# Attention with float32 scores on half arrays and V as the stationary operand, from inputs that the host lays out

## Chip, cores and metric

One core of one Trainium2 chip runs the whole program. The metric is the device time of one execution in microseconds. The engines are TensorE (PE; PEld is its weight load), VectorE (DVE), ScalarE (ACT), GpSimd (POOL) and SyncE (SP), whose queue issues the transfers.

## What is computed

Attention with a block-causal mask over 8 batches of 8 heads, 576 tokens of 64 columns, then a soft mixture of experts over the 4608 tokens, then a wide layer with squared ReLU whose weights are float64.

```python
scores = scale * np.matmul(q, k.transpose(0, 1, 3, 2))      # (8, 8, 576, 576)
mask = block_i >= block_j                                   # blocks of 64 tokens
scores = np.where(mask, scores, -1000000000.0)
attn = np.exp(scores - np.max(scores, axis=-1, keepdims=True))
attn = attn / (np.sum(attn, axis=-1, keepdims=True) + 1e-09)
x = np.matmul(attn, v)                                      # then to (4608, 512)
x = _moe_ref(x=x, **moe_kwargs)
return _moe2_ref(x=x, **moe2_kwargs)
```

## The kernel before

Attention goes over 32 pairs of heads (p), four pairs a batch. A pair's two heads lie on the two halves of the partitions, 64 columns each. A plan written out by hand sets the order: `SLOT` gives each step a time in a pair's own clock of 8 units (L24), the steps of all pairs are sorted by 8p plus that time, and each engine executes its part of the sorted list in order (`run`, L608). A step that waits therefore holds all that stands behind it on its engine.

The steps of a pair. `load` (L228) brings q and k in rows and v (eight transfers for q and k, three for v). `t_kq` transposes q and k on TensorE, ten transposes of 128 columns (L274). `c_kq` copies them on ScalarE rounded to float32r (KQ, L282), and `d_kq` keeps what the rounding lost on VectorE (KQL, L287). `rough` (L298) computes scores from the rounded parts alone and `rough_max` (L307) takes each row's maximum on VectorE; `m_row` (L325) transposes the maxima and two transfers put them into one row per head, MR. `score` (L370) goes over four chunks `CH` of key blocks and query columns (448, 448, 320+128 and 192+128 columns a head); each chunk takes four single passes: high by high, high by low, low by high, and NEG by MR, which subtracts the maxima and sets masked entries. `expo` takes the exponential on ScalarE (L384), `p_hi` a float16 part of it on ScalarE, `p_lo` the float16 remainder on GpSimd (L391). `v_scale` and `split_v` scale V by a power of two and split it in two float16 parts (L333, L349). `pv` (L407) multiplies in three float16 products for each block of 128 queries, 128 keys and head, 90 in all, with the weights as the stationary operand and V, with a column of ones for the sums, streaming. `norm` (L421) divides on VectorE. `route_t` and the routing steps of a batch (L445 to L553) follow with transposes and small float32 products.

The banks: scores and rough scores share two buffers of two banks in turn (`ps_s`), transposes, maxima and routing share two single banks (`ps_t`), and there is one buffer of two banks for the weights times V (`ps_v`).

After the last pair come the last batch's routing, the experts while the float64 weights are converted, and the wide layer, from L620 on. Their weights go into buffers that lie where the attention's tiles lay.

## Time and profile before

| what | us |
|---|---|
| median of 3 runs (971.98 to 978.46) | 974.12 |
| the profiled execution: its span | 974.9 |
| TensorE busy in it | 877.6 |
| VectorE busy | 699.4 |
| ScalarE busy | 599.5 |
| GpSimd busy | 286.1 |

The profiled execution has no time of its own beside its span, which is the time from its first to its last instruction. Busy times are averages over stages with different limits. A row of the timeline gives start and length; since matmuls are pipelined, the distance between two starts is what one costs and the length is what its result takes. A float32 product (not float32r) has two records on TensorE.

### The profile page before, as it was taken

What the parts mean: (1) busy time and instruction counts of PE and PEld (TensorE: products, weight loads), DVE (VectorE), ACT (ScalarE), POOL (GpSimd) and SP (SyncE); (2) the same over time, 40 slices, a digit from 0 to 9 for tenths busy, and PEclk for the clock granted to TensorE, in tenths of its full rate; (3) what the DMA queues carried; (4) which work ended last, traced back from release to release, by engine and by line L of the source; (5) the groups of instructions that cost most, each with busy time, mean ns of one, the idle gap of its engine ahead of it and who ended that gap; (6) DMA issues with size and microseconds to landing.
All of it is one profiled execution on the core that took longest, in us unless ns stands there. A gap on an engine that the chain in (4) does not pass through costs nothing.

```text
span 974.9 us, 20485 instructions
## 1 busy us (share of the span) xinstructions
PE 877.6 (90%) x8052; PEld 519.8 (53%) x8052; DVE 699.4 (72%) x1277; ACT 599.5 (61%) x1025; POOL 286.1 (29%) x224
## 2 busy tenths in 40 slices
PE   3899989988899989976857799999999999999998
PEld 2677767767677767763111344444444444444443
DVE  5798979878798979857978776565555565565553
ACT  2677767767677857774457565555555565555553
POOL 6476746656466656670100000000000000000000
PEclk9999999999999999996879799999999999999999
DMA  4544543535244424255998000001000100010001
GB/s 112 127 92 117 132 113 71 133 101 123 65 122 124 124 57 124 70 215 196 414 403 326 1 1 33 33 1 34 33 1 33 33 33 1 33 33 1 34 33 32
DMA packets 150927, 91.73 MB, mean 94 GB/s; under 512 B 127472, under 2 KB 127792, under 8 KB 150832
## 3 DMA queue, kind: packets, MB, share of 16 engines
q1 hardware_dynamic: 150832, 90.44, 30.8%
q8 instruction: 63, 1.03, 0.4%
q14 instruction: 32, 0.26, 0.1%
HBM read 80.81 MB, written 9.44 MB: 93 GB/s over the span
## 4 chain that ended last, share of the span: by engine, by line
PE 43%; DVE 7%; ACT 2%; issue 1%; DVEq 0%; ACTq 0%
PE o L1044 13%; PE o L1042 13%; PE o L1043 13%; PE h L1014 3%; DVE cvg L637 2%; DVE cve L644 1%; DVE cvg L636 1%; ACT cvl L728 1%; DVE cvl L645 1%; DVE wi L762 1%; DVE cvg L724 1%; PE h L657 0%; ACT wo_0s L745 0%; ACT cvg L633 0%; DVE wo_6s L750 0%
## 5 line engine op out<-in xcount | busy, mean ns | idle before, releaser
L263 POOL TENSOR_TENSOR pl<-pc,ph 128x896 f16<-128x896 f32 (+1 forms) x128 | 232.8, 1820 | 153.8 <-ACT ph L256 81.0
L1022 DVE SCALAR_TENSOR_TENSOR g<-r,sk 128x384 f32<-128x384 f32 x192 | 119.5, 622 | 126.0 <-ACT r L1016 124.4
L1016 ACT ACTIVATE r<-h,fo 128x384 f32<-128x384 f32 x192 | 111.3, 580 | 155.2 <-PE h L1014 154.0
L384 ACT ACTIVATE pc<-s 128x896 f32<-128x896 f32 (+1 forms) x128 | 110.7, 865 | 79.0 <-PE s L379 49.6
L1030 DVE SCALAR_TENSOR_TENSOR rl<-g,bk,rh 128x384 f16<-128x384 f32 x192 | 118.2, 615 | 8.9 <-ACT rh L1028 7.7
L1028 ACT ACTIVATE rh<-g,bk 128x384 f16<-128x384 f32 x192 | 116.2, 605 | 0.2 <-DVE g L1022 0.2
L256 ACT CAST ph<-pc 128x896 f16<-128x896 f32 (+1 forms) x128 | 113.4, 886 | 4.1
L293 DVE TENSOR_REDUCE mm<-s 128x2 f32<-128x1024 f32 (+3 forms) x128 | 101.9, 818 | 10.0 <-PE s L304 9.6
L780 POOL TENSOR_TENSOR c<-lgs,mc 128x192 f32<-128x192 f32 x6 | 3.7, 612 | 352.8 <-DVE mc L778 352.8
L417 PE MATMUL pv<-vh,ph 128*128 128x65 f16 x960 | 103.0, 197 | 1.3 <-DVE xt L433 1.3
L419 PE MATMUL pv<-vh,pl 128*128 128x65 f16 x960 | 101.5, 194 | 1.4 <-POOL pl L263 1.4
L418 PE MATMUL pv<-vl,ph 128*128 128x64 f16 x960 | 101.8, 194 | 0.0
L417 PEld LDWEIGHTS <-ph 128*128 128x128 f16 x960 | 86.9, 98 | 23.4 <-issue 6.4
L1044 PEld LDWEIGHTS <-rl 128*128 128x128 f16 x576 | 56.4, 98 | 68.9 <-DVE rl L1030 1.0
L1042 PEld LDWEIGHTS <-rh 128*128 128x128 f16 x576 | 56.5, 98 | 66.5 <-issue 0.3
L419 PEld LDWEIGHTS <-pl 128*128 128x128 f16 x960 | 88.9, 98 | 1.6 <-POOL pl L263 1.5
L418 PEld LDWEIGHTS <-ph 128*128 128x128 f16 x960 | 88.9, 99 | 0.0
L1043 PEld LDWEIGHTS <-rh 128*128 128x128 f16 x576 | 56.5, 98 | 58.2 <-issue 0.6
L263 DVE TENSOR_TENSOR kql<-tp,kq 128x512 fp32r<-128x512 f32 (+1 forms) x96 | 57.5, 600 | 30.2 <-ACT kq L285 29.2
L269 PE MATMUL tp<-idF,rqk 128*128 128x128 f32 x320 | 58.5, 301 | 22.0 <-DVE kql L263 9.6
L304 PE MATMUL s<-kq 64*128 64x64 f32 (+4 forms) x384 | 55.9, 338 | 19.8 <-DVE me L293 13.8
L379 PE MATMUL s<-mr,neg 64*128 64x128 f32 (+3 forms) x384 | 66.7, 318 | 6.7 <-DMA mr<-mT 6.5
(229 smaller groups left out, 1963.6 us busy)
## 6 DMA issues: line engine op xcount, KB each, us to landing
w<-in_moe_w_dram SPq DMA_DIRECT2D x36, 512.0 KB
w2h<-in_moe_w_dram SPq DMA_DIRECT2D x28, 512.0 KB
rqk<-in_k_dram SPq DMA_DIRECT2D x64, 128.0 KB
rqk<-in_q_dram SPq DMA_DIRECT2D x64, 128.0 KB
rv<-in_v_dram SPq DMA_DIRECT2D x64, 128.0 KB
wi<-in_moe_w_in_dram SPq DMA_DIRECT2D x8, 1024.0 KB
wo<-in_moe_w_out_dram SPq DMA_DIRECT2D x8, 1024.0 KB
out_dram<-ob SPq DMA_DIRECT2D x32, 256.0 KB
```

The costliest lines, as they stand in the source:

```text
L256: ACT.copy(o, i)
L263: eng.tensor_tensor(out=o, in0=i, in1=h, op=ALU.subtract)
L417: PE.matmul(o, a, vh[:, 2 * sl + h, 0:65], start=(c == 0 and n == 0), stop=False)
L418: PE.matmul(o[:, 0:64], a, vl[:, 2 * sl + h, :], start=False, stop=False)
L419: PE.matmul(o, l, vh[:, 2 * sl + h, 0:65], start=False, stop=(c == 3 and n == len(UNIT[c]) - 1))
L1016: ACT.activation(out=r, in_=hps, func=AF.Relu, scale=fo[:, 0:1])
L1022: DVE.scalar_tensor_tensor(out=g0, in0=r, scalar=sk[:, f:f + 1], in1=r, op0=ALU.mult, op1=ALU.mult)
L1028: ACT.activation(out=rh, in_=g0, func=AF.Identity, bias=bk[:, f:f + 1])
L1030: DVE.scalar_tensor_tensor(out=rl, in0=g0, scalar=bk[:, f:f + 1], in1=rh, op0=ALU.add, op1=ALU.subtract)
L1042: PE.matmul(o, rh[:, 128 * i:128 * i + 128], hl[f][0], start=(f == 0), stop=False)
L1043: PE.matmul(o, rh[:, 128 * i:128 * i + 128], hl[f][1], start=False, stop=False)
L1044: PE.matmul(o, rl[:, 128 * i:128 * i + 128], hl[f][0], start=False, stop=(f == 15))
```

## The change

The host passes k and q transposed, two heads on 128 rows and 640 columns, and v with its rows in place and zeros at the end, so that each is one transfer. The transposes of q and k, both remainders, the scaling and the splits go. q and k are rounded to float32r by ScalarE for the rough scores alone (`round_kq`). The scores are one float32 product on the unrounded data and the NEG by MR pass. V in float32 is the stationary operand, 64 columns for each head, and the float32 weights stream; the two heads write the two halves of the output's partitions. The result, columns by tokens, is copied out by ScalarE (`pv_out`), transposed on TensorE (`tokens`), and `norm` divides it. The sums of the weights over the key blocks are made on GpSimd (`key_sum`), split in two float16 parts by ScalarE and GpSimd (`sum_hi`, `sum_lo`), and summed over the keys by products with a column of ones (`dens`). The plan has new times.

```diff
 SLOT = {
-    "ld_k": -28.8, "ld_q": -28.6, "ld_v": -18.0,
-    "t0": -17.0, "c0": -16.98, "d0": -16.97, "t1": -15.2, "c1": -15.1, "d1": -15.05, "t2": -13.2, "c2": -13.1, "d2": -13.0,
+    "ld_k": -17.7, "ld_q": -17.6, "ld_v": -10.0, "rd_k": -13.6, "rd_q": -13.4,
     "r0": -11.8, "x0": -11.6, "r1": -9.8, "x1": -9.6, "r2": -7.8, "x2": -7.6, "r3": -5.8, "x3": -5.6,
-    "m_row": -3.2, "vs0": -9.3, "vs1": -5.1, "sv0": -4.5, "sv1": -2.5,
+    "m_row": -3.2,
     "s0": 0, "e0": 0.1, "s1": 2, "e1": 2.1, "s2": 4, "e2": 4.1, "s3": 6, "e3": 6.1,
-    "h0": 0.3, "h1": 2.3, "h2": 4.3, "h3": 6.3, "l0": 0.5, "l1": 2.5, "l2": 4.5, "l3": 6.5,
-    "pv0": 4.7, "pv1": 6.7, "pv2": 8.7, "pv3": 10.7, "norm": 10.9,
+    "a0": 0.3, "a1": 2.3, "a2": 4.3, "a3": 6.3, "sh0": 4.6, "sh1": 8.3, "sl0": 6.4, "sl1": 8.4,
+    "pv0": 2.7, "pv1": 4.7, "pv2": 6.7, "pv3": 8.7, "oc": 8.9, "tb0": 10.75, "tb1": 11.3, "den": 11.35, "norm": 11.4,
...
     def load(p, nm):
...
+        t = {"k": KT, "q": QT, "v": RV}[nm][p % 3]
+        SP.dma_start(out=t, in_={"k": k, "q": q, "v": v}[nm][p // 4, p % 4])
...
-    def t_kq(p, x):
-    def c_kq(p, x):
-    def d_kq(p, x):
+    def round_kq(p, nm):
+        o, i = (KR, KT) if nm == "k" else (QR, QT)
+        cp(RND[nm], o[p % 2], i[p % 3])
...
-        [(3, 384, 576, 0), (4, 448, 576, 192)],
+        [(3, 384, 576, 0), (4, 512, 576, 192)],
...
     def score(p, c):
-            for n, (a, b) in enumerate([(t[:, 0, ks], t[:, 1, qs]), (t[:, 0, ks], l[:, 1, qs]), (l[:, 0, ks], t[:, 1, qs]),
-                                        (NEG[:, sl, :], mr[:, qs])]):
+            for n, (a, b) in enumerate([(kt[:, ks], qt[:, qs]), (NEG[:, sl, :], mr[:, qs])]):
                 for h in range(2):
...
+    def key_sum(p, c):
+        pc = st["pc", p, c]
+        if c == 0:
+            return
+        if c == 1:
+            S = st["S", p] = ring("S", [128, 2, 448], F32)
+            POOL.tensor_tensor(out=S, in0=st["pc", p, 0], in1=pc, op=ALU.add)
+            return
+        S = st["S", p]
+        for sl, c0, c1, o in CH[c]:
+            if sl:
+                x = S[:, :, c0 - 128:c1 - 128]
+                POOL.tensor_tensor(out=x, in0=x, in1=pc[:, :, o:o + c1 - c0], op=ALU.add)
+
+    def sum_hi(p, part):
...
+            ACT.copy(st["sh", p][:, :, 0:128], st["pc", p, 2][:, :, 320:448])
...
+            ACT.copy(st["sh", p][:, :, 128:576], st["S", p])
+
+    def sum_lo(p, part):
...
+            lo(POOL, st["sl", p][:, :, 128:576], st.pop(("S", p)), st["sh", p][:, :, 128:576])
...
     def pv(p, c):
+        pc, rv = st["pc", p, c], RV[p % 3]
+        for sl, c0, c1, o in CH[c]:
+            head = sl == 0
+            x = (1, slice(0, c1)) if c1 <= 128 else (0, slice(c0 - 128, c1 - 128))
+            for h in range(2):
+                r = slice(64 * h, 64 * h + 64)
+                PE.matmul(st["pv", p][r, x[0], x[1]], rv[:, sl, r], pc[:, h, o:o + c1 - c0],
+                          start=head, stop=(sl == 4 or c1 <= 128))
+
+    def pv_out(p):
+        o, ps = ring("ot", [128, 576], F32), st.pop(("pv", p))
+        ACT.copy(o[:, 0:128], ps[:, 1, 0:128])
+        ACT.copy(o[:, 128:576], ps[:, 0, 0:448])
...
+    def tokens(p, part):
+        ot = st["ot", p]
+        ps = st["tb", p, part] = ps_t.tile([128, 512], F32, tag="tp", name="tp")
+        for n, u in enumerate(range(4) if part == 0 else (4,)):
+            tr(ps[:, 128 * n:128 * n + 128], ot[:, QS[u]:QS[u] + 128], idF)
+
+    def dens(p):
+        ps = st["tb", p, 1]
+        sh, sl = st.pop(("sh", p)), st.pop(("sl", p))
+        for u in range(5):
+            for h in range(2):
+                for n, x in enumerate((sh, sl)):
+                    PE.matmul(ps[:, 128 + 2 * u + h:129 + 2 * u + h], x[:, h, QS[u]:QS[u] + 128], ones_h[:, 0:1],
+                              start=(n == 0), stop=(n == 1))
...
-    at(-60, 0, build_zero)
...
+def _lay_k(a):
+    a = a.transpose(0, 1, 3, 2)
+    b, h, d, n = a.shape
+    a = a.reshape(b, h // 2, 2 * d, n)
+    return _concat([a, a[..., n - 64:]])
```

## Rows read from the trace of the kernel before

**Rows 1.** Attention's stretch: us; PE, PEld, DVE, ACT, POOL busy (instructions); clock; DMA share, GB/s.

```profile
0.00:437.18 437.18, 381.00 (x5653) 303.00 (x5653) 360.37 (x680) 303.19 (x482) 273.17 (x205) 0.98 0.44 111
```

**Rows 2.** The same columns for a regular pair and for the last pair.

```profile
281.03:292.67 11.64, 10.45 (x172) 8.69 (x169) 10.88 (x19) 9.12 (x15) 8.10 (x5) 1.00 0.37 84
...
428.87:437.18 8.31, 5.85 (x125) 5.12 (x121) 2.12 (x5) 5.77 (x8) 7.04 (x5) 1.00 1.02 414
```

**Rows 3.** Line L430 (norm): duration ns, first and last start.

```profile
L430 DVE TENSOR_TENSOR xb<-pv,rr x32: 691/692/692, 47.0 to 437.2; 128x512 f32<-128x512 f32 x32
```

**Rows 4.** Timeline of TensorE in a regular pair: start, us, line, tiles, shape, count.

```profile
275.46 0.82 PE L379 MATMUL s<-mr,neg 64*128 64x448 f32 x2
276.79 0.52 PE L304 MATMUL s<-kq 64*128 64x192 f32 x4 [0.50 <-DVE me L293]
277.24 0.20 PE L417 MATMUL pv<-vh,ph 128*128 128x65 f16 x1
...
277.98 0.63 PE L269 MATMUL tp<-idF,rqk 128*128 128x128 f32 x4
278.54 0.47 PE L379 MATMUL s<-kq 64*128 64x448 f32 x2
278.84 0.36 PE L379 MATMUL s<-kql,kq 64*128 64x448 f32 x2
...
279.46 0.19 PE L304 MATMUL s<-kq 64*128 64x64 f32 x2
...
281.34 0.28 PE L379 MATMUL s<-kq,kql 64*128 64x128 f32 x2
281.45 0.27 PE L379 MATMUL s<-mr,neg 64*128 64x128 f32 x2
281.94 0.50 PE L304 MATMUL s<-kq 64*128 64x512 f32 x2 [0.21 <-ACT kq L285]
```

**Rows 5.** Waits from 200 to 400 us: total, times, longest.

```profile
PE s L304 <- DVE me L293: 6.8, 9, 1.0
```

**Rows 6.** Timeline of TensorE: float32 products on 32 output columns, and what follows.

```profile
253.17 1.07 PE L516 MATMUL tp<-xb,d 128*32 128x512 f32 x8
254.06 1.02 PE L519 MATMUL tp<-xt,d 128*32 128x512 f32 x2
255.01 0.47 PE L379 MATMUL s<-kq 64*128 64x448 f32 x2
```

**Rows 7.** Groups of instructions, shapes apart: busy us, mean ns, idle before.

```profile
L263 POOL TENSOR_TENSOR pl<-pc,ph 128x896 f16<-128x896 f32 x96 | 182.1, 1898 | 129.5 <-ACT ph L256 64.8 <-issue 42.6 <-PE tp L269 9.4
L256 ACT CAST ph<-pc 128x896 f16<-128x896 f32 x96 | 90.2, 939 | 3.1
...
L357 DVE SCALAR_TENSOR_TENSOR vl<-rv,al,vh 128x640 f16<-128x640 f32 x32 | 64.7, 2021 | 1.0 <-POOL vh L354 1.0
...
L285 ACT CAST kq<-tp 128x512 fp32r<-128x512 f32 x64 | 36.8, 576 | 21.6 <-PE tp L269 21.1
```

**Rows 8.** Timeline of ScalarE in the same pair.

```profile
274.07 0.73 ACT L256 CAST ph<-pc 128x640 f16<-128x640 f32 x1
274.70 0.73 ACT L337 ACTIVATE sq<-rv 128x640 bf16<-128x640 f32 x1
...
279.72 0.92 ACT L384 ACTIVATE pc<-s 128x896 f32<-128x896 f32 x1 [0.49 <-PE s L304]
```

**Rows 9.** Timeline of VectorE at the start: the last mask copy and what follows.

```profile
13.78 1.52 DVE L224 CAST mr<-xb 64x640 fp32r<-64x640 f32 x2 [1.47 <-POOL xb L216]
15.34 1.29 DVE L263 TENSOR_TENSOR kql<-tp,kq 128x512 fp32r<-128x512 f32 x2
```

**Rows 10.** Timeline of TensorE at the start: the first pass with the maxima.

```profile
29.22 1.59 PE L379 MATMUL s<-mr,neg 64*128 64x448 f32 x2 [1.28 <-DMA mr<-mT]
```

**Rows 11.** Timeline of SyncE's queue: the row of maxima.

```profile
273.23 1.50 SPq L331 DMA_DIRECT2D mr<-mT  x2
```

**Rows 12.** Timeline of TensorE at the end of an odd batch.

```profile
350.96 0.66 PE L269 MATMUL tp<-idF,rqk 128*128 128x128 f32 x4 [2.02 <-ACT lp L494]
```

More of the change, by code (lines that the diff above doesn't have):

```diff
@@ L34 @@
 }
-PH = "AAAA"
-PL = "PPPP"
-LN256 = 5.545177444479562
+RND = {"k": "A", "q": "A"}
+PEXP = 16.0
+LNP = 2.772588722239781
 @with_exitstack
@@ L58, in fused_kernel @@
     PE, ACT, DVE, POOL, SP = nc.tensor, nc.scalar, nc.vector, nc.gpsimd, nc.sync
-    B, H, S, D = q.shape
+    B, D, S, H = q.shape[0], q.shape[2] // 2, q.shape[3] - 64, 2 * q.shape[1]
     NB = B
@@ L118, in fused_kernel @@
     idH = const.tile([128, 128], F16, name="idH")
-    ones_b = const.tile([128, 128], BF16, name="ones_b")
+    ones_h = const.tile([128, 2], F16, name="ones_h")
     I8 = const.tile([128, 64], F32, name="I8")
@@ L176, in fused_kernel @@
     ps_v = rt.enter_context(tc.tile_pool(name="ps_v", bufs=1, space=PSUM))
-    VH = [latep.tile([128, 10, 66], F16, name=f"vh_{i}") for i in range(3)]
     MX = [latep.tile([128, 128], F32R, name=f"mx_{i}") for i in range(2)]
@@ L182, in fused_kernel @@
     ME = [latep.tile([128, 2, 5], F32, name=f"me_{i}") for i in range(2)]
-    RS = [latep.tile([128, 2, 5], F32, name=f"rs_{i}") for i in range(2)]
+    RS = [latep.tile([128, 10], F32, name=f"rs_{i}") for i in range(2)]
     def load_const():
@@ L409, in pv @@
             st["pv", p] = ps_v.tile([128, 2, 512], F32, tag="pv", name="pv")
-        vh, vl = VH[p % 3], st["vl", p]
-        ph, pl = st.pop(("ph", p, c)), st.pop(("pl", p, c))
-        for h in range(2):
-            for n, (u, sl, off) in enumerate(UNIT[c]):
-                o = st["pv", p][:, h, 65 * u:65 * u + 65]
-                a, l = ph[:, h, off:off + 128], pl[:, h, off:off + 128]
-                PE.matmul(o, a, vh[:, 2 * sl + h, 0:65], start=(c == 0 and n == 0), stop=False)
-                PE.matmul(o[:, 0:64], a, vl[:, 2 * sl + h, :], start=False, stop=False)
-                PE.matmul(o, l, vh[:, 2 * sl + h, 0:65], start=False, stop=(c == 3 and n == len(UNIT[c]) - 1))
+        pc, rv = st["pc", p, c], RV[p % 3]
@@ new lines, in fused_kernel @@
+    QS = [128 * u for u in range(4)] + [448]
+    def tokens(p, part):
[11 more added lines that the diff above has]
+                              start=(n == 0), stop=(n == 1))
@@ new lines, in norm @@
+        rr = ring("rr", [128, 5, 2, 1], F32)
+        DVE.reciprocal(out=rr.rearrange("p u h a -> p (u h a)"), in_=r)
+        xo = XB[:, :, 128 * j:128 * j + 128].rearrange("p u (h c) -> p u h c", h=2)
+        DVE.tensor_tensor(out=xo, in0=t0.rearrange("p (u h c) -> p u h c", u=4, h=2),
+                          in1=rr[:, 0:4].to_broadcast([128, 4, 2, 64]), op=ALU.mult)
+        xt = XT[l0:l0 + 64, 128 * j:128 * j + 128].rearrange("p (h c) -> p h c", h=2)
+        DVE.tensor_tensor(out=xt, in0=t1[64:128, 0:128].rearrange("p (h c) -> p h c", h=2),
+                          in1=rr[64:128, 4].to_broadcast([64, 2, 64]), op=ALU.mult)
@@ L436, in gt @@
+        for c in range(4):
+            st.pop(("pc", p, c))
+        st.pop(("ot", p))
     def gt(b, i=0):
@@ L568, in fused_kernel @@
             A("ld_" + nm, load, nm)
-        for x in range(3):
-            A(f"t{x}", t_kq, x)
-            A(f"c{x}", c_kq, x)
-            A(f"d{x}", d_kq, x)
+        for nm in "kq":
+            A("rd_" + nm, round_kq, nm)
         for r in range(4):
@@ L583, in fused_kernel @@
             A(f"e{c}", expo, c)
-            A(f"h{c}", p_hi, c)
-            A(f"l{c}", p_lo, c)
+            A(f"a{c}", key_sum, c)
             A(f"pv{c}", pv, c)
+        for x in range(2):
+            A(f"sh{x}", sum_hi, x)
+            A(f"sl{x}", sum_lo, x)
+            A(f"tb{x}", tokens, x)
+        A("oc", pv_out)
+        A("den", dens)
         A("norm", norm)
@@ L1092, with _lay_q, _lay_v, _concat @@
 _OUTS = [((4608, 512), 'float32')]
+def _lay_k(a):
[3 more added lines that the diff above has]
+    return _concat([a, a[..., n - 64:]])
+def _lay_q(a):
+    a = a.transpose(0, 1, 3, 2)
+    b, h, d, n = a.shape
+    a = a.reshape(b, h // 2, 2 * d, n)
+    return _concat([a[..., :64], a])
+def _lay_v(a):
+    b, h, n, d = a.shape
+    o = np.zeros((b, h // 2, 640, 2, d), a.dtype)
+    o[:, :, :n] = a.reshape(b, h // 2, 2, n, d).transpose(0, 1, 3, 2, 4)
+    return np.ascontiguousarray(o.reshape(b, h // 2, 5, 128, 2 * d).transpose(0, 1, 3, 2, 4))
+def _concat(parts):
+    return np.ascontiguousarray(np.concatenate(parts, axis=-1))
+_LAY = {"q": _lay_q, "k": _lay_k, "v": _lay_v}
 def kernel(**inputs):
```

133 lines of the change are left out of this document (27 added, 106 removed).

## Prediction

> **What bounds the kernel now.** I read first the busy time of the attention stage, then single pairs, then one pair on TensorE, and last who waits for whom. Attention runs to 437.2 us of the 974.9; the change touches no code after it, so I leave those 537.7 us as they are. The reader is to see that in this stage, 32 pairs of heads, TensorE is busy 381 and VectorE 360 us [rows 1], and that neither has room: in a regular pair of 11.64 us TensorE is busy 10.45 and VectorE 10.88 [rows 2]. The normalisation runs once per pair, first at 47.0 and last at 437.2 [rows 3], so 31 intervals make 390.2 us. Of these 28 have the regular pair's length plus what a batch adds, and the last three are shorter, down to 8.31 [rows 2], for no rough maxima and transposes of a next pair are left.
>
> On TensorE the pair has 10.1 us of work and two waits. The rough scores that should follow the last pass at 275.46 start at 276.79, 1.1 us later than a pass's 0.2 us would give, and VectorE releases them; the ones at 281.94 come 0.4 us late [rows 4]. Over 200 us the VectorE wait stands at 6.8 us, longest 1.0 [rows 5]. So the pair is TensorE's work plus waits for a VectorE that is itself full.
>
> **TensorE's work after the change.** All float32 prices come from products that write 32 of the 128 output columns: four products of 512 columns, two records each, take 0.89 us (253.17 to 254.06), one alone 0.95 with what follows it [rows 6]. So a record of 512 columns streams 0.43 us, a product takes two records, and products on different column parts of the array run side by side. Per column that is 1.67 ns a product: 448 columns 0.75, 320 columns 0.54, 192 columns 0.32, 128 columns 0.22 us. I take the same overlap for two halves of the array; what happens otherwise is the first rival.
>
> Scores: a chunk of 448 columns now takes 0.92 us (278.54 to 279.46), 0.30 for the first pass and 0.20 for each other [rows 4]; after the change 0.10 exposed load, 0.75 and 0.20, together 1.05. For the other two a pass of 320 columns counts 0.15 by its columns and a narrow one 0.11 (281.34 to 281.45), which I take for 64 columns too. The chunk of 320 and 128 then stays at 1.12, the last, 192 and 64 instead of 192 and 128, goes from 0.97 to 0.86. Sum: +0.15.
>
> Weights times V: 24 products take 0.74 us (277.24 to 277.98) [rows 4], so 90 take 2.75. After: columns 448, 448, 320+128 and 192+64, so 0.75, 0.75, 0.76 and 0.43, 2.7 us, plus for each chunk a load that nothing hides and a change of the array's shape. The first pass of a score chunk is 0.1 us longer than the others, and at 255.01 the next shape starts 0.09 us after the float32 stream before it should end (254.06 and two records of 0.43) [rows 4, 6]; I take 0.15 for both (from nothing to 0.3). Sum 3.3: +0.55.
>
> Transposes: ten of q and k (0.56 for four [rows 4]) and the sum of squares go, 1.5 us; five of the output come (0.7) and 20 products of one column at 0.03 each, as the old products (0.6); with a change of shape 1.4: -0.05. Together 10.1 + 0.65 = 10.8 us: TensorE gets no relief.
>
> **The other engines.** VectorE loses the low half of V, 2.0 us [rows 7], and three remainders, 0.65 each for the wide ones [rows 9], some 4 of 10.88 us, and stops being late with what is left. ScalarE: from 9.1 to about 7.2 us. GpSimd: an 896-wide sum costs 1.90 us [rows 7]; with widths 896, 640, 384, 128, 256 and 896, at the same price per element (2.1 ns), 6.8 us, and 7.4 with an estimated 0.1 for each start. It fits in place of the 8.1 of today [rows 2]. Loads: one transfer instead of eight for q and k and three for v; the queue has less to issue and I count no gain.
>
> **The new waits.** Now ScalarE's order counts: weights of chunk 0, high half of the last pair's sums (896 wide), then the two copies that free the one output bank, and TensorE needs that bank for chunk 0 of the weights times V. From the end of the scores: 0.26 until ScalarE starts (279.46 to 279.72), then the chain. A ScalarE operation that doesn't read the one before starts about 0.1 us before its end (274.07 + 0.73 against 274.70) [rows 4, 8]. So 0.83 for the weights (0.92 long), 0.85 for the high half (0.94 [rows 7]), 0.15 and 0.53 for copies of 128 and 448 columns (a copy of 512 takes 0.58 [rows 7]), 0.06 back: 2.7 us. In this time TensorE has rough scores (0.45), the last weights times V (0.58), must wait for the weights of chunk 0 until 1.24, and does scores (1.05) and rough scores (0.12): 2.4. It waits 0.2 and 0.3, so the pair takes 10.8 + 0.5 = 11.3 us, 0.35 less than 11.64. Behind the waiting product stand the transposes, the sums' products and the scores of chunk 2. The sums' low half on GpSimd (1.90 after the high half, done 3.8 us after the scores) is read 4.25 us after them: hidden, by under half a us, and every tenth it is later costs a tenth. The row of maxima: two issues take 1.5 us [rows 11] and the data are there some 1.8 us after the second; they go out 2 us before the next pair's scores and are read 0.85 into these: hidden by about 0.4 us.
>
> **The sum.** 28 pairs at -0.35: -9.8. Batches: at the end of an odd one TensorE waits 2.0 us for ScalarE before it may reuse a transposes' bank [rows 12]; afterwards the transpose of the exponentials waits for the same chain: 0. The last pairs: no rough maxima as before, but the last pair must sum (1.5), halve (0.9), take the remainder (1.9) and multiply where it split once before (0.7 and 1.4): +3.4. The start: VectorE is held by the masks until 15.3 [rows 9], and today two pairs' remainders and halves of V then follow, so that the second score pass with the maxima ends at 30.8 [rows 10]. Without them: four rough maxima (4.6), transpose and copy (0.7), two issues and landing (3.4): about 24. I take -7.5 for start and first pair, since the first pair has no earlier output to copy. After attention: the weight buffers that lie where K and V lay are freed later, hidden behind the last batch's routing; +1. Together -12.9 on the profiled 974.9: 962.0. The runs' median is 974.12, 0.8 lower: 961.
>
> **Rivals.** (1) The halves of the array don't run float32 products at the same time. For: no row has one on half the rows, and each product is two records. Against: column parts do [rows 6], and the single-pass halves do (a pair of 448 columns in 0.20 us) [rows 4]. Price: scores alone 2.8 us a pair more, weights times V alone 2.7: the waits of 0.5 us absorb next to nothing of it, as they lie elsewhere, so 31 pairs give +84, about 1045, or both 1130. It decides as soon as one of the two is serial. This is the case on the other side.
>
> (2) The shape of the array is the cost. The change goes through three shapes in a pair, ten changes for eight. By the rows a change costs 0.09 us and this is in the sum. If each chunk of weights times V instead pays the tail of the product before it and of its own (a pass is recorded for 0.37 us and repeats every 0.20 [rows 4]), that is 0.3 more per chunk, 1.2 a pair of which 0.2 falls into waits: 12.3 us, +31, about 990. The Trainium skill, TensorEngine Tiling (Array Packing), section Tiling Modes, says that changing the mode, not just the tile, drains the engine. By that rule this rival holds in full wherever the shape changes; the trace shows only the 0.09 us.
>
> (3) GpSimd's sums are late: with float32 output at 2.5 us for 1.9, the remainder ends 0.2 after it is needed, and its wide sums hold up the next high half. Price 0.5 us a pair: about 977.
>
> (4) The waits vanish and loads hide: 10.8 us or less a pair, 945 and below.
>
> **How the numbers follow.** My forecast has 0.64. With the chunk price from nothing to 0.3 its pair takes 10.9 to 11.8 us, so 945 to 980 with the start's bounds, likeliest 961. Rival 1: 0.13, rival 2: 0.13, rival 3: 0.05, rival 4: 0.05. From 940 to 1000 stand my forecast, rivals 2 and 3 and some of 4, a little over 8 in 10; rival 1 and the rest of 4 are left out. Faster than 964.4, over 1%, which is about what a measurement tells here from no change: 0.41 of mine and rival 4, 0.46. Within 1% up to 983.9: 0.23 of mine, most of rival 3: 0.27. Slower: rivals 1 and 2, 0.27 with the rest of 3.
>
> **What would show it.** Score passes in float32 of two heads starting together, 0.37 us for 448 columns a record; pairs of 11.3 us; VectorE near 7 us a pair; TensorE waiting for ScalarE's output copies and not for VectorE; the first normalisation near 39.5. Records of one head after the other, or a product that starts only when the tail before it ends, would make the prediction wrong, as would TensorE waiting for GpSimd or for the row of maxima.

## The result, and the profile after

The kernel after takes 946.78 us, median of 4 runs (946.0 to 947.53); beside it before took 975.24 (971.98 to 978.46). The ratio is 0.970, 95% interval 0.967 to 0.973: 28 us faster, where 13 were forecast. The profiled execution of after spans 944.2 us, that of before 974.9.

The windows of after, with the columns of [rows 1]: attention up to the last normalisation, a regular pair, the last pair, and an odd batch's long interval.

```profile
0.00:406.40 406.40, 371.88 (x3605) 232.52 (x3605) 264.76 (x489) 224.18 (x386) 255.37 (x229) 1.00 0.34 115
247.74:258.64 10.90, 10.54 (x104) 6.71 (x102) 7.55 (x14) 6.59 (x11) 7.57 (x7) 1.00 0.28 92
396.60:406.40 9.80, 7.00 (x74) 4.95 (x70) 2.07 (x6) 5.99 (x9) 7.21 (x7) 0.84 0.54 198
311.83:328.63 16.80, 15.06 (x159) 9.11 (x157) 9.62 (x25) 7.78 (x16) 7.80 (x7) 1.00 0.19 60
```

TensorE is busy as long as before, 10.54 of 10.90 us where it was 10.45 of 11.64 [rows 2]. VectorE has gone from 10.88 to 7.55 us. The normalisation, the line that answers to [rows 3], runs from 39.2 to 406.4 instead of from 47.0 to 437.2; what lies behind it is unchanged, 537.8 us for 537.7.

```profile
L390 DVE TENSOR_TENSOR xb<-tp,rr x32: 690/692/692, 39.2 to 406.4; 128x512 f32<-128x512 f32 x32
```

TensorE's timeline in that regular pair, which answers to [rows 4]. Twenty products with a column of ones (L378) are left out: they start 0.025 us apart, from 252.93 to 253.40.

```profile
247.74 1.02 PE L309 MATMUL s<-qt,kt 64*128 64x448 f32 x4
248.24 0.71 PE L309 MATMUL s<-mr,neg 64*128 64x448 f32 x2
248.80 0.42 PE L264 MATMUL s<-kr,qr 64*128 64x192 f32 x4
249.15 0.66 PE L354 MATMUL pv<-pc,rv 128*64 128x192 f32 x8
250.00 1.02 PE L309 MATMUL s<-qt,kt 64*128 64x448 f32 x4 [0.19 <-ACT pc L314]
250.50 0.72 PE L309 MATMUL s<-mr,neg 64*128 64x448 f32 x2
251.06 0.20 PE L264 MATMUL s<-kr,qr 64*128 64x64 f32 x2
251.42 0.97 PE L354 MATMUL pv<-pc,rv 128*64 128x448 f32 x4 [0.17 <-ACT ot L360]
252.32 0.77 PE L245 MATMUL tp<-idF,ot 128*128 128x128 f32 x5
...
253.50 0.81 PE L309 MATMUL s<-qt,kt 64*128 64x320 f32 x4
```

A chunk of 448 columns takes 1.06 us by its starts (247.74 to 248.80): two heads, two records each, and the pass with the maxima. Weights times V take 0.90 (251.42 to 252.32). Two waits are left, for the weights that free the score bank (250.00) and for the output copies (251.42). The chain behind the second is seen on ScalarE:

```profile
249.03 0.92 ACT L314 ACTIVATE pc<-s 128x896 f32<-128x896 f32 x1 [1.74 <-PE s L309]
249.84 0.93 ACT L336 CAST sh<-S 128x896 f16<-128x896 f32 x1
250.67 0.27 ACT L359 COPY ot<-pv 128x128 f32<-128x128 f32 x1
250.82 0.55 ACT L360 COPY ot<-pv 128x448 f32<-128x448 f32 x1
```

TensorE's longest waits from 200 to 400 us (total, times, longest), where [rows 5] had 6.8 us for VectorE's maxima: that line is gone.

```profile
PE pv L354 <- ACT ot L360: 2.4, 11, 0.7
PE tp L245 <- ACT lp L458: 2.4, 2, 1.2
PE s L309 <- ACT pc L314: 1.5, 8, 0.2
```

The difference of the two profiled executions, by intervals between normalisations:

| stretch | before | after | difference | forecast |
|---|---|---|---|---|
| start to the first normalisation | 47.0 | 39.2 | -7.8 | -7.5 |
| 21 regular intervals | 249.3 | 229.9 | -19.4 | -7.4 |
| 4 at the end of even batches | 55.2 | 56.7 | +1.5 | -1.4 |
| 3 at the end of odd batches | 57.8 | 50.4 | -7.4 | -1.0 |
| last 3 intervals | 27.9 | 30.3 | +2.4 | +3.4 |
| behind attention | 537.7 | 537.8 | +0.1 | +1 |

The forecast's 28 pairs at -0.35 are put on their three kinds here. So the regular pairs and the odd batches hold the miss. The times add to 30.7 us here, the difference of two executions, where the medians differ by 28.5.

### The profile page after: what moved, and what is told of

Its sections match the earlier page's. It is cut to its first block, busy times and chain, and to the rows that moved or that the text cites. A ratio compares the mean times of both kernels' runs of the same rounds, so it can differ in the third digit from the quotient of the medians.

```text
span 944.2 us, 15561 instructions
## 1 busy us (share of the span) xinstructions
PE 866.9 (92%) x6004; PEld 448.1 (47%) x6004; DVE 603.7 (64%) x1085; ACT 519.5 (55%) x929; POOL 268.7 (28%) x248
## 4 chain that ended last, share of the span: by engine, by line
PE 44%; DMA 4%; DVE 4%; ACT 1%; issue 1%; SPq 0%; DVEq 0%
PE o L1004 13%; PE o L1005 13%; PE o L1006 13%; PE h L976 3%; DMA w<-in_moe_w_dram 3%; DMA w2h<-in_moe_w_dram 1%; DVE cvg L599 1%; ACT cvl L690 0%; DVE cve L606 0%; DVE cvg L686 0%; DVE cvg L598 0%; PE h L619 0%; DVE cvl L607 0%; DVE wi L724 0%; ACT cvg L595 0%
## 5 line engine op out<-in xcount | busy, mean ns | idle before, releaser
L309 PE MATMUL s<-qt,kt 64*128 64x448 f32 (+4 forms) x768 | 133.0, 431 | 3.8 <-ACT pc L314 3.5
L329 POOL TENSOR_TENSOR S<-S,pc 128x640 f32<-128x640 f32 (+2 forms) x96 | 95.8, 998 | 83.3 <-ACT pc L314 78.1
L354 PE MATMUL pv<-pc,rv 128*64 128x448 f32 (+4 forms) x768 | 115.0, 407 | 4.1 <-ACT ot L360 4.1
L309 PE MATMUL s<-mr,neg 64*128 64x448 f32 (+4 forms) x384 | 95.6, 490 | 0.0
L239 POOL TENSOR_TENSOR sl<-S,sh 128x896 f16<-128x896 f32 x32 | 60.6, 1893 | 47.5 <-ACT sh L336 47.5
L309 PEld LDWEIGHTS s<-qt,kt 64*128 64x128 f32 x768 | 59.7, 187 | 27.5 <-ACT pc L314 9.4
L323 POOL TENSOR_TENSOR S<-pc 128x896 f32<-128x896 f32 x32 | 66.9, 2090 | 18.4 <-ACT pc L314 18.4
L264 PE MATMUL s<-kr,qr 64*128 64x64 f32 (+4 forms) x384 | 52.5, 320 | 18.3 <-DVE mm L253 9.0
L976 PE MATMUL h<-ct,mst 128*128 128x384 f16 x192 | 62.7, 329 | 3.8 <-DVE mst L955 3.8
L354 PEld LDWEIGHTS pv<-pc,rv 128*64 128x64 f32 x768 | 43.8, 136 | 36.3 <-issue 12.9
L1004 PE MATMUL o<-wo_0s,rh 128*128 128x512 f16 x144 | 55.3, 384 | 0.0
L1005 PE MATMUL o<-wo_0s,rh 128*128 128x512 f16 x144 | 55.1, 383 | 0.0
```

The lines of the kernel that those rows point to most:

```text
L309: PE.matmul(ps[:, h, o:o + c1 - c0], a[r], b[r], start=(n == 0), stop=(n == 1))
L329: POOL.tensor_tensor(out=x, in0=x, in1=pc[:, :, o:o + c1 - c0], op=ALU.add)
L354: PE.matmul(st["pv", p][r, x[0], x[1]], rv[:, sl, r], pc[:, h, o:o + c1 - c0], start=head, stop=(sl == 4 or c1 <= 128))
L1004: PE.matmul(o, rh[:, 128 * i:128 * i + 128], hl[f][0], start=(f == 0), stop=False)
L1005: PE.matmul(o, rh[:, 128 * i:128 * i + 128], hl[f][1], start=False, stop=False)
```

## Experiments

The theory: before was TensorE's work plus waits for a full VectorE; the change gives TensorE no relief, and the gain is VectorE's time. The rivals: TensorE's own work or the transfers gained it; and, for what the forecast missed, a collision on SyncE's queue and the clock at the odd batches. Ratios are to before on the same chip; differences against after are to its 946.78 us, some of them from another chip (the medians of before lie at 973.8 to 977.5 us).

**VectorE relieved in before.** Edit: `vl`, the low half of V, is computed for two pairs and used again.

```diff
...
+        elif p >= 2:
+            st["vl", p] = VL[p % 2]
...
```

> The kernel before, but the low half of V is computed for the first two pairs only and used again for all later ones, so 30 of 32 pairs leave out that remainder (2.0 us of VectorE each); TensorE, ScalarE and GpSimd keep all their work. Theory A: before, the pair of 11.64 us is 10.1 us of TensorE work plus waits for a VectorE that is full (10.88 us). With 8.9 us of VectorE the waits go and the pair falls to 10.3 to 10.6 us: -28 to -37 us, about 942. Rival: the pair is set by TensorE's own work or by ScalarE, and VectorE is just as busy beside it: at most -10 us, pairs at 11.3 or more.

Measured: 958.91 us, ratio 0.986 (0.982 to 0.990), -15.8. The window of a regular pair, and one line of TensorE's waits over attention:

```profile
271.90:282.70 10.80, 10.31 (x175) 8.22 (x173) 8.61 (x20) 8.38 (x13) 7.93 (x6) 1.00 0.40 91
```

```profile
PE pv L420 <- DVE xt L436: 6.7, 19, 1.6
```

One VectorE operation of 2.0 us on average is gone, and the pair is 0.84 us shorter (10.80 for 11.64) with TensorE's work untouched. Both the pair and the 15.8 us lie beyond what the rival allowed (11.3 and 10). They fall short of the theory's 10.3 to 10.6 and 28, because the next wait came up: the weights times V now stand 0.35 us on average (6.7 us in 19 times) for a normalisation that VectorE does in order behind the rest.

**VectorE loaded again in after.** Edit: four differences of 128x640 a pair, results unused.

```diff
...
+        DVE.tensor_tensor(out=t, in0=i, in1=i, op=ALU.subtract)
...
```

> The kernel after with four VectorE operations of 128x640 added per pair (results unused), at the places where before computed remainders and low halves. By the price of 0.69 us for 512 columns they take about 0.86 us each, 3.4 us a pair: VectorE goes from 7.5 to 10.9 us of the 10.9 us pair. Theory A: what the change gains is VectorE's time; TensorE again waits for maxima and the pair rises to 11.6 us or more: +20 to +35 us. Rival: the change gains by TensorE's work and the loads, VectorE has slack: less than +8 us.

Measured: 1075.05 us, ratio 1.103: +128 against after, far beyond both. The operations did not take 0.86 us. Groups of VectorE in attention (busy us, mean ns, idle before):

```profile
L255 DVE TENSOR_TENSOR dum<-rv 128x640 f16<-128x640 f32 x128 | 166.8, 1303 | 3.0
L287 DVE TENSOR_TENSOR mx<-mm,me 128x10 fp32r<-128x10 f32 x32 | 46.5, 1452 | 1.1
```

Their shortest was 0.81, their longest 2.60 us, and the maximum of ten numbers took 1.45. What they have in common is two inputs in SBUF. Two rows of after, from VectorE's timeline and from GpSimd's, show when such a maximum ends:

```profile
251.63 1.13 DVE L282 TENSOR_TENSOR mx<-mm,me 128x10 fp32r<-128x10 f32 x1
```

```profile
250.84 1.90 POOL L239 TENSOR_TENSOR sl<-S,sh 128x896 f16<-128x896 f32 x1 [1.26 <-ACT sh L336]
```

It ends at 252.76, and GpSimd's at 252.74. The low half of V in before, in the pair of [rows 2], shows the same for a longer operation:

```profile
284.47 2.50 DVE L357 SCALAR_TENSOR_TENSOR vl<-rv,al,vh 128x640 f16<-128x640 f32 x1
```

```profile
284.38 1.90 POOL L263 TENSOR_TENSOR pl<-pc,ph 128x896 f16<-128x896 f32 x1
```

It starts 0.09 us after GpSimd's operation and ends 0.69 us behind its end; in 8 of the 32 pairs it took only 0.87 to 0.89. So a new theory: a VectorE operation with two inputs in SBUF that starts while GpSimd works stands until GpSimd's operation ends, and does its own work then. The trace of the run with the four differences bears it out: the 56 of the 128 that start with no GpSimd operation under way take 0.81 to 0.83 us, and the 72 others all end 0.68 to 0.69 us behind the GpSimd operation that was under way, 0.90 to 2.60 us after their start. The Trainium skill, SBUF — State Buffer, section Who interferes with whom, says that a VectorE instruction with two SBUF inputs contends with a GpSimd instruction that reads SBUF, and that one with at most one SBUF input does not, some modes of VectorE aside. The next run puts the inputs to the test.

**The same load with one input.** Edit, against the run above: the four differences become maxima over the same 640 columns, with five results a row in place of 640.

```diff
...
-        DVE.tensor_tensor(out=t, in0=i, in1=i, op=ALU.subtract)
+        DVE.tensor_reduce(out=t, in_=RV[p % 3], axis=AX, op=ALU.max)
...
```

> The kernel after with four VectorE operations per pair at the same places and over the same 640 columns as in the run that cost 128 us, but maxima with one input in place of differences with two. Theory: there the differences did not take 0.9 us but up to 2.6, since each stood until a GpSimd operation ended; maxima take 0.85 us each wherever they stand, VectorE comes to 10.9 us a pair as in before, and the cost is 20 to 45 us. Rival: the place of the operations and not their inputs is what cost the time: again 100 us or more.

Measured: 980.61 us, ratio 1.004 (1.002 to 1.006): +34 against after. The operation's group, the window of a regular pair, and TensorE's longest wait from 200 to 400 us:

```profile
L254 DVE TENSOR_REDUCE dum<-rv 128x5 f32<-128x640 f32 x128 | 104.8, 819 | 3.0
```

```profile
265.00:276.80 11.80, 11.03 (x103) 6.75 (x103) 9.84 (x18) 6.69 (x12) 7.66 (x7) 1.00 0.25 84
```

```profile
PE s L268 <- DVE mm L257: 8.0, 12, 1.4
```

Place and columns read were those of the run before, and 94 us are gone. The operation and its output differ besides the inputs, but the differences themselves took 0.81 to 0.83 us wherever they started with GpSimd idle. Part of the 94 us is the clock: over attention TensorE's granted clock was 0.90 with the differences and 0.98 with the maxima. And with VectorE loaded to 9.84 us, under its load in before, after loses all that the change had gained, while the transfers and TensorE's products stay as they are in after: the pair is 11.8 us, TensorE again waits for maxima, and the 21 regular intervals take 250.1 us (249.3 in before, 229.9 in after). So the gain in the regular pairs is VectorE's time.

VectorE's 10.88 us in before were not all work, though. In that pair the low half of V stood 1.6 us for GpSimd (2.50 for 0.87), right ahead of the maxima for which TensorE waited. Whether before gains as much when this operation is only moved out of GpSimd's way was not tried.

**Scores split again in after.** Edit: `score` takes three float32r products with remainders of q and k that VectorE computes; the host's layout, the float32 weights times V and the sums stay. The buffers change with it: two for three of q and k, three for two of the rounded ones.

```diff
...
+        lo(DVE, o[p % 2], i[p % 2], r[p % 3].bitcast(F32))
...
-            for n, (a, b) in enumerate([(kt[:, ks], qt[:, qs]), (NEG[:, sl, :], mr[:, qs])]):
+            for n, (a, b) in enumerate([(kt[:, ks], qt[:, qs]), (kt[:, ks], ql[:, qs]), (kl[:, ks], qt[:, qs]), (NEG[:, sl, :], mr[:, qs])]):
```

> The kernel after with its scores in three single-pass products again, as in before: VectorE computes the two remainders of q and k (128x640 each; 640 columns at the 0.69 us for 512 make 0.86 each, more where GpSimd is in the way), the layout by the host, the float32 weights times V and the sums on GpSimd stay. Theory: the float32 scores as such gave nothing, TensorE's chunk is 0.92 us by either way against 1.06 now, and VectorE has 3.4 us free of 10.9; so the time stays within 8 us of after's 947. Rival: the float32 scores are a good part of the gain because they free VectorE: the remainders bring waits back and cost 12 us or more.

Measured: 960.58 us, ratio 0.987 (0.984 to 0.989): +14 against after, the rival's side. A window of 11.4 us, a regular pair and 0.2 us more:

```profile
243.20:254.60 11.40, 11.04 (x118) 7.85 (x119) 10.03 (x17) 6.68 (x11) 7.69 (x6) 1.00 0.57 180
```

The regular pair is 11.2 us though each chunk of 448 columns is 0.14 us cheaper on TensorE. So about half of the gain comes with the float32 scores. But the regular pairs do not wait for maxima here. TensorE waits for GpSimd's remainder of the sums, which takes 2.48 us for 1.90 where VectorE's remainder of k began 0.09 us before it: this time it is GpSimd that stands for VectorE (timelines of VectorE and GpSimd, and TensorE's waits from 200 to 400 us):

```profile
248.88 0.83 DVE L241 TENSOR_TENSOR kl<-kt,kr 128x640 fp32r<-128x640 f32 x1
```

```profile
248.97 2.48 POOL L241 TENSOR_TENSOR sl<-S,sh 128x896 f16<-128x896 f32 x1 [1.11 <-ACT sh L342]
```

```profile
PE tp L384 <- POOL sl L241: 2.2, 11, 0.2
```

The intervals at the ends of batches grew as well, from 13.9 to 14.8 us and from 16.8 to 18.2, and are part of the 14.

**Both heads' scores on one half of the array.** The second head is computed from the first head's data, so its result is left out.

```diff
...
-                    r = slice(64 * h, 64 * h + 64)
+                    r = slice(0, 64)
...
```

> The kernel after with the score products of both heads on the upper half of the array's rows (the second head is then computed from the first head's k and q, so its result is left out); all product counts and sizes are the same. It prices the first rival of the prediction. If halves of the array run float32 products at the same time, as the records of after suggest, taking that away costs 0.75 us for a chunk of 448 columns and 0.2 for its single pass with the maxima, about 3.2 us a pair: pairs of 13.9 to 14.2 us, +85 to +105 us. If the records only look as if they overlap, the time stays within 10 us.

Measured: 1072.48 us, ratio 1.101, +126. TensorE's timeline there (compare 250.00 to 251.06 above):

```profile
283.02 1.77 PE L309 MATMUL s<-qt,kt 64*128 64x448 f32 x4 [0.16 <-ACT pc L314]
284.26 0.29 PE L264 MATMUL s<-kr,qr 64*128 64x64 f32 x1
284.28 0.91 PE L309 MATMUL s<-mr,neg 64*128 64x448 f32 x2
285.04 0.19 PE L264 MATMUL s<-kr,qr 64*128 64x64 f32 x1
285.16 0.97 PE L354 MATMUL pv<-pc,rv 128*64 128x448 f32 x4
```

The chunk goes from 1.06 to about 2.0 us and the median pair from 10.91 to 14.31: +3.4, against 3.2 expected. The first rival of the prediction was priced about rightly, at 2.8 us a pair, and it did not happen: in after the halves do run float32 products side by side. The total went past the range because the start lost 18 us as well (the first normalisation at 57.4): there each such group of four records is 3.35 us long instead of 1.77, at a granted clock of 1.00. Why is not known; in after too the first two such groups are longer, 1.87 us for 1.02.

**The load ahead of a row of maxima.** In before one regular interval is 15.6 us. There the transfer of the row of maxima is issued right behind 1 MB of weights, and TensorE waits for it (SyncE's timeline and TensorE's, of before):

```profile
201.79 0.60 SPq L106 DMA_DIRECT2D wi<-in_moe_w_in_dram  x1
202.49 1.50 SPq L331 DMA_DIRECT2D mr<-mT  x2
```

```profile
207.97 0.68 PE L379 MATMUL s<-mr,neg 64*128 64x448 f32 x2 [3.50 <-DMA mr<-mT]
```

Two edits of before's plan for these loads, one for each run:

```diff
-        at(10 + 234 * i / NPRE, 10, load_w, wseq[i], wpre[i])
+        at(10.5 + 234 * i / NPRE, 10, load_w, wseq[i], wpre[i])
```

```diff
-        at(10 + 234 * i / NPRE, 10, load_w, wseq[i], wpre[i])
+        at(8 * ((10 + 234 * i / NPRE) // 8) + 5.2, 10, load_w, wseq[i], wpre[i])
```

> The kernel before with the loads of the weights for the end of the kernel issued half a unit later in the plan, so that none is issued just ahead of a row of maxima; nothing else is changed. Theory: the one interval of 15.6 us (pair 12; TensorE waits 3.9 us there for the row of maxima, whose transfer stands behind a 1 MB load of weights) falls to about 11.7: -4 us, 0.4%, and the total of TensorE's waits for these rows over attention falls from 11.7 to under 8 us. Rival: the long interval has another cause, or the collision moves to another pair: within 1 us of before.

> The kernel before with each load of weights planned right behind a pair's row of maxima, so that none can be issued between the row's being ready and its transfer (half a unit later left the load just ahead of the same row). Theory: the interval of 15.6 us becomes 11.7, -3 to -5 us. Rival: the load is not what held the row; the long interval stays and the time is within 1.5 us of before.

Measured: 975.10 us (ratio 1.000, 0.998 to 1.003) and 972.47 us (0.995, 0.993 to 0.998). In the first the load still went out just ahead of the same row (201.5 and 202.2) and the interval stayed at 14.9: the edit did not do what it was for, and says nothing of the theory. In the second the interval is 11.5 us and TensorE's waits for these rows over attention fall from 6.5 to 2.5 us:

```profile
PE s L379 <- DMA mr<-mT: 2.5, 6, 1.4
```

The one long interval is 4.1 us shorter in that trace, so some 4 of the 28 us are this collision. In after it does not occur; the longest wait there for such a row is 0.7 us.

**The odd batches.** In before TensorE waits 2.02 us [rows 12], in after 1.19, both for ScalarE's copies of the logits. Most of the 0.83 us is again VectorE standing for GpSimd: on this chain an operation of 32 numbers with two inputs in SBUF took 0.78 us in before, to the end of GpSimd's (1.00 and 1.01 in the other two batches), and 0.27 to 0.28 in after.

```profile
349.15 0.78 DVE L486 SCALAR_TENSOR_TENSOR nrun<-mt,nrun 32x1 f32<-32x1 f32 x1
```

```profile
348.53 1.40 POOL L263 TENSOR_TENSOR pl<-pc,ph 128x640 f16<-128x640 f32 x1 [1.84 <-ACT ph L256]
```

Two edits move the wait: in after one VectorE difference is put ahead of the second maximum; in before (and later in after) ScalarE's copies go ahead of the exponentials, for which they need not wait.

```diff
...
+                DVE.tensor_tensor(out=dum, in0=rv, in1=rv, op=ALU.subtract)
             rmax(mt, pt)
...
```

> The kernel after with one VectorE operation of 128x640 (result unused, some 0.9 us) ahead of the second maximum in the odd batches 1, 3 and 5, on the chain for which TensorE waits 1.2 to 1.4 us there. Theory: in before this wait of 2.0 us was followed by products at the lower clock, in after it is shorter and the clock stays; with the operation TensorE waits about 2.1 us, the granted clock falls behind it, and the interval goes from 16.8 to 18.5 to 19.3 us. Rival: the clock has nothing to do with the shorter interval; it grows by the 0.9 us alone, to 17.7 at most.

```diff
+        ACT.copy(lp[:, 0:128], ps[:, 0:128])
...
         ACT.activation(out=ex[:, 0:128], in_=ps[:, 0:128], func=AF.Exp, bias=nn)
...
-        ACT.copy(lp[:, 0:128], ps[:, 0:128])
...
```

> The kernel before with ScalarE's copies of the logits ahead of the exponentials: TensorE's wait of 2.02 us at the end of an odd batch falls to about 1.6. Theory: if the lower clock is brought by the length of this wait, some of the three odd batches keep the full clock and their interval falls from 19.3 to 17.3 (0.4 for the wait, 1.5 for the clock), -2 to -6 us in all. Rival: the wait's length does not decide; the clock falls as before and each interval loses 0.4 at most: -1 to -3 us with the even batches.

Measured: 956.01 us (+9 against after) and 969.93 us, ratio 0.994 (0.992 to 0.997). Windows from the end of the wait to the next normalisation, the first of before (2.02 us waited), the second of before with the copies first (1.45); the third fence has the three whole intervals of after with the added operation (2.37):

```profile
248.22:257.76 9.54, 9.48 (x97) 6.89 (x99) 5.48 (x15) 5.29 (x9) 1.89 (x1) 0.82 0.12 27
```

```profile
242.29:250.30 8.01, 7.96 (x97) 5.58 (x99) 5.38 (x15) 5.44 (x10) 1.89 (x1) 1.00 0.16 37
```

```profile
120.22:139.71 19.49, 16.56 (x159) 9.88 (x157) 10.77 (x26) 8.04 (x17) 8.36 (x7) 0.91 0.20 61
218.89:238.44 19.55, 16.62 (x159) 9.95 (x157) 10.77 (x26) 7.82 (x17) 8.37 (x7) 0.91 0.19 57
318.45:339.46 21.01, 18.08 (x159) 10.29 (x156) 10.77 (x26) 7.78 (x16) 8.36 (x7) 0.84 0.16 48
```

The same products take 9.54 us at a mean granted clock of 0.82 and 8.01 at 1.00: 1.5 us for the lower of the two levels (1.2 GHz for 2.4). In before the clock falls behind all three waits; with the copies first behind none, and the intervals go from 19.2 and 19.3 to 17.5 and 17.2. In after it falls behind none until the wait is lengthened, and then behind all three. So of the 2.5 us by which after's odd intervals are shorter, 1.5 are the clock and 0.8 the wait. The length alone does not decide: with 2.02 us waited the clock stayed in two of three in the run without V's low half and in one of three in the run with the loads behind the row, and with only 1.19 us waited it fell in one of three (0.85; 22.0 us for 20.5) in the run with both heads on one half.

**Versions of after.** Two waits are left in a pair. First the order on ScalarE: output copies ahead of the sums' high half; then the same with the sums' products (12.25 in the plan for 11.35), the normalisation (12.3 for 11.4) and the routing (14.908 for 13.708, its transposes 14.1 for 12.9) later.

```diff
-    "a0": 0.3, "a1": 2.3, "a2": 4.3, "a3": 6.3, "sh0": 4.6, "sh1": 8.3, "sl0": 6.4, "sl1": 8.4,
+    "a0": 0.3, "a1": 2.3, "a2": 4.3, "a3": 6.3, "sh0": 4.6, "sh1": 8.95, "sl0": 6.4, "sl1": 9.0,
```

> The kernel after with the two copies of the output bank placed ahead of the high half of the sums on ScalarE (only the order of the two changes). Theory: TensorE's first product of weights times V no longer waits for the copies (0.24 us), but the remainder of the sums on GpSimd starts 0.7 us later and the sums' products wait for it: pairs of 11.4 to 11.7 for 10.9, +14 to +22 us. Rival: the sums have slack: -3 to -8 us.

> As the run with the copies first, and the sums' products, the normalisation and the transposes of the routing are planned later, behind the next scores, so that the remainder of the sums on GpSimd has 0.9 units of the plan (about 1.2 us) more. Theory: then nothing waits for GpSimd, TensorE no longer waits for the copies, and the pair falls from 10.9 to 10.6 to 10.7 us: -5 to -10 us against after, 937 to 942. Rival: the wait for the weights of chunk 0 or another takes the place of the one removed: within 3 us of after.

Measured: 957.21 us (+10; pair 11.28) and 981.30 us (+35; pair about 11.5). TensorE's waits from 200 to 400 us, one line of each:

```profile
PE tp L378 <- POOL sl L239: 5.2, 12, 0.5
```

```profile
PE tp L243 <- DVE xb L390: 6.3, 16, 0.4
```

The first is as expected in kind: GpSimd's remainder, started 0.7 us later, held TensorE by 0.4 us, so it had less than half a us of slack, as the prediction said. In the second the theory failed: the transpose of the next pair's maxima shares its two banks with the sums and now waits for the late normalisation. Some 23 of the 35 us lie at the batches: most even intervals take 15.7 us for 13.9, the ones right behind a batch 12.7 for 10.2 to 10.9, the odd ones 17.7 for 16.8; why was not followed.

Next TensorE's order: the second part of chunk 2 of weights times V goes behind the next pair's first scores, into the wait at 250.00 above; then besides it the copies first and the remainder of 896 on VectorE (the second diff, with its step at 10.35 in the plan).

```diff
...
+                A("pv2", pv, 2, 0)
+                at(max(z + 8.65, -50), 0, pv, p, 2, 1)
...
```

```diff
-            lo(POOL, st["sl", p][:, :, 128:576], st.pop(("S", p)), st["sh", p][:, :, 128:576])
+            lo(DVE, st["sl", p][:, :, 128:576], st.pop(("S", p)), st["sh", p][:, :, 128:576])
```

> The kernel after with one change of order on TensorE: the second part of chunk 2 of weights times V (two products of 128 columns, 0.32 us) is issued behind the next pair's first score chunk instead of ahead of it. There TensorE now stands 0.36 us for the score bank that the weights of chunk 0 set free. Theory: the scores start 0.32 us earlier, the part fills the wait, and the pair falls from 10.9 to 10.6 us: -7 to -11 us against after. Rival: the earlier scores wait for their bank (the weights of the last chunk end about when they would start) and the hole only moves: within 2 us of after.

> As the run with the part of chunk 2 behind the scores, and besides the output copies stand ahead of the sums' high half on ScalarE and the sums' remainder of 896 is VectorE's instead of GpSimd's (512 columns took 0.69 us there, so some 1.2 us for 1.9). Theory: TensorE waits neither for the copies nor for the remainder, VectorE goes from 7.5 to 8.7 us and keeps slack: pairs of 10.3 to 10.5, -12 to -18 us against after. Rival: the remainder holds up the maxima behind it on VectorE, or stands behind GpSimd's sums: no better than the run without it, or worse.

Measured: 943.92 us, ratio 0.966 (0.963 to 0.969), and 956.74 us, 0.979. The first fills the hole (pair 10.69), but the regular intervals right behind an even batch, 10.2 us in after, become 10.7, and with a few longer ones the 21 together gain only 1.2 us; the even intervals gain 3.5, and one odd one loses 1.6 to the lower clock. A difference from after is not shown. In the second TensorE's transpose of the maxima waits, and VectorE's group shows for what:

```profile
PE tp L243 <- DVE xb L390: 3.3, 9, 0.4
```

```profile
L282 DVE TENSOR_TENSOR mx<-mm,me 128x10 fp32r<-128x10 f32 x32 | 49.1, 1534 | 1.1
```

The maximum of ten numbers again: it lasts until GpSimd's first sum ends (1.62 us, 0.03 behind it), and the normalisation stands behind it. So two more edits: logits first, as above; and this maximum taken over one tile with the two sets interleaved, one input for two.

```diff
-            DVE.tensor_tensor(out=MX[p % 2][:, 0:10], in0=mm.rearrange("p h j -> p (h j)"),
-                              in1=ME[p % 2].rearrange("p h j -> p (h j)"), op=ALU.max)
+            rmax(MX[p % 2][:, 0:10], MM[p % 2].rearrange("p h j t -> p (h j) t"))
```

After unchanged, then the part later with logits first, then this with the one-input maximum, then all of it with the copies first and VectorE's remainder:

> The kernel after once more, unchanged, on the same chip as the next two. Expected: 944 to 949, odd batches of 16.8 with TensorE's wait of 1.2 us and the full clock.

> The kernel after with the second part of chunk 2 of weights times V behind the next scores, and with ScalarE's copies of the logits ahead of the exponentials, for which they do not wait. Theory: the pair is 10.7 us for 10.9 (-0.2 x 28 = -5), the wait at the end of an odd batch falls from 1.4 by the copies' 0.4 to about 1.0 us and the lower clock is not seen there: -5 to -10 us against after, 937 to 942. Rival: the copies first hold up the exponentials of the pairs, or other waits take over: within 2 us of after, or slower.

> As the run with the part of chunk 2 later and the logits first; the maximum that ends a pair's rough maxima is taken by a reduction over one tile (one input) instead of from two tiles. Theory: a VectorE operation with two inputs in SBUF stands until GpSimd's operation ends, one with one input does not; the operation falls from a mean of 1.1 us to under 0.3, the pair stays at 10.7 since nothing on TensorE waits for it: within 3 us of the 943 without this edit. Rival: it keeps its 1 us, so the inputs are not the reason.

> As the run with the sums' remainder on VectorE and the copies first (956.7), with the logits first and the maximum with one input. Theory: there the maximum stood 1.6 us for GpSimd's first sum, the normalisation started late and TensorE's transpose of the maxima waited 0.35 us for it; without that the pair falls from 11.1 to 10.4 to 10.7 and the time to 936 to 946. Rival: the remainder on VectorE is itself too much; pairs stay at 11 us and the time above 950.

| run | us | ratio (95%) |
|---|---|---|
| after again | 946.55 | 0.971 (0.967 to 0.975) |
| part later, logits first | 943.22 | 0.967 (0.964 to 0.971) |
| the same, one-input maximum | 945.38 | 0.969 (0.966 to 0.971) |
| and copies first, remainder on VectorE | 937.97 | 0.963 (0.960 to 0.965) |

In the last one, the groups of VectorE's two operations, and the normalisation's row:

```profile
L238 DVE TENSOR_TENSOR sl<-S,sh 128x896 f16<-128x896 f32 x32 | 34.9, 1090 | 28.1 <-ACT sh L334 28.1
L252 DVE TENSOR_REDUCE mx<-mm 128x10 fp32r<-128x20 f32 x32 | 5.6, 174 | 1.1
```

```profile
L388 DVE TENSOR_TENSOR xb<-tp,rr x32: 690/692/693, 38.9 to 396.6; 128x512 f32<-128x512 f32 x32
```

With one input the maximum takes 0.17 us for 1.53, and the kernel that was slower by 10 us than after is faster by 9, of which the logits' order gives some: many pairs take 10.4 us. The one-input maximum alone changes nothing, as expected, since there nothing on TensorE waits for it. The last version beats both kernels; its interval lies below that of after, 0.967 to 0.973.

## Why the prediction was wrong, and what in it was right

The forecast was 13 us, the gain 28. The step that failed is TensorE's work in a pair after the change: the prediction summed it to 10.8 us, and the trace has 10.30. So a regular pair gained 0.73 us and not 0.35, which makes 8 us more over the 21 regular intervals. Two smaller steps failed beside it: the odd batches at 0, where 7.4 us were gained, and 28 intervals all taken as the regular one, where one of 15.6 us lost 4 us of its own. The mechanism, VectorE's time, was right.

- **What bounds the kernel: right, with one thing unseen.** TensorE's work plus waits for VectorE. Relieving VectorE in before gave 15.8 us; loading it again in after took 34, more than the whole gain. But VectorE was not "itself full" of work: of its 10.88 us, 1.6 went by while the low half of V stood for GpSimd.
- **TensorE gets no relief: right in kind, mis-sized.** The prices of the new products held: 1.06 for the chunk of 448 (forecast 1.05), 0.90 for weights times V (0.90). What failed is the sum of the small terms, 10.8 us. Measured, the pair's starts give 10.30: sums' products and output transposes 1.18 for 1.40, scores 3.98 for 4.08, weights times V 3.20 for 3.30, and 0.08 on the rest. Each of the four was put too high by a tenth or two, and together they made half a us a pair.
- **The new waits: right.** The chain from the scores' end to the first weights times V took 2.62 us for 2.7; the waits came to 0.60 us (0.36 and 0.24) for 0.5. So the pair took 10.9 us for 11.3, the lower end of the forecast's own 10.9 to 11.8.
- **28 regular pairs at 11.64: failed by one.** The 15.6 us interval was in the trace and was not asked about; the change took it away and with it 4 us.
- **Odd batches 0: failed.** "The transpose of the exponentials waits for the same chain" was right, but the chain is shorter (1.19 us for 2.02, mostly as VectorE stands less for GpSimd in it), and the lower clock behind it was not in the sum: 7.4 us in three batches, 4.5 of them the clock. The even ones took 1.5 us more where 1.4 less were forecast.
- **Start, last pairs, after attention:** -7.8 for -7.5, +2.4 for +3.4, +0.1 for +1: right. The start is right by its steps as well: the first pass with the maxima ended at 23.5 us, where about 24 was forecast.
- **Rivals.** One: did not happen; its price of 2.8 us a pair was 3.4 when forced. Two: each chunk of weights times V took no more than its columns and the 0.15 us in the sum for load and change of shape together (0.90 for 0.75), so the 0.3 us more of this rival are not there; the Trainium skill's draining (TensorEngine Tiling (Array Packing), section Tiling Modes) is not seen in any row as more than that 0.15. Three: GpSimd's sum with float32 output took 2.09 us for the 1.9 or 2.5 considered, and its remainder held TensorE only in runs where it started 0.7 us later or itself stood for VectorE. Four, at most 945 with all waits gone: the time came within 2 us of it, but with 0.60 us of waits in each pair, so not by this rival's way.
- **Marks.** VectorE near 7 us: 7.55, of which 1.0 is the maximum of ten numbers standing for GpSimd. First normalisation near 39.5: 39.2. Waits for output copies and not for maxima: seen. The direction was right, and the time lies at the lower end of the stated 945 to 980.

What stays open: what beside the length of TensorE's wait decides whether the lower clock follows it; what before would gain if the low half of V were only moved out of GpSimd's way; and why the intervals at and behind a batch grew in the versions with another order.

## To carry to other kernels

When an engine off the critical path is nearly full, price a change by what it takes from that engine as well, and test it by loading the engine again: the whole gain should go. Before a forecast multiplies a regular interval, explain every irregular one in the trace (here 15.6 and 19.3 for 11.6), for the change may remove its cause. An operation whose duration is far above that of its size, like 1.1 us for ten numbers, may be a wait in disguise; see which other engine's operation ends with it, or ends before it by just the time that the work itself takes.

## What was unexpected in the hardware

- A VectorE operation with two inputs in SBUF that starts while a GpSimd operation is under way stands until that ends, and then takes its own time: ten numbers 1.07 us on average in after, ending 0.02 to 0.03 us behind GpSimd, and 0.17 with one input; 640 columns up to 2.60 us, ending 0.68 to 0.69 behind, and 0.81 to 0.83 when they started with GpSimd idle. Where VectorE's operation began first, by 0.09 us, GpSimd's stood: 2.48 us for 1.90. The wait is recorded as busy time: VectorE's 10.88 us in before [rows 2] hold 1.6 of it, in the low half of V, which took 2.50 us there and 2.0 on average [rows 7].
- VectorE need not be full to be the bound: 9.84 of 11.80 us were enough to bring TensorE's waits back, since its operations come in order.
- Behind TensorE's wait of about 2 us at an odd batch the granted clock mostly fell to the lower level and cost 1.5 us: in 9 of 12 cases behind 2.02 us (before and three edits of it), in 1 of 6 behind 1.40, in 1 of 15 behind 1.19 (after, once more, and three edits), and in none of 9 behind 0.83 (the three versions with the logits first).
